# Second MLP of a linear-attention block: x forms kept in an SBUF ring, second-layer weights stored column-permuted, last sums combined in PSUM, other step places

## The chip, the core and the metric

The kernel runs on one core of a Trainium2 chip. The metric is device microseconds of one execution. TensorE (PE) does the matrix work, VectorE (DVE) and ScalarE (ACT) empty PSUM and do elementwise work, GpSimd (POOL) does elementwise work in SBUF, and SyncE (SP) issues nearly all DMAs.

## The reference

```python
x = attention(q, k, v)                         # linear attention, 4608 tokens x 512
x = (relu(x @ moe_w_in) ** 2) @ moe_w_out      # first MLP, 512 -> 2048 -> 512
h = x @ moe2_w_in                              # second MLP, same sizes
g = h * (1.0 / (1.0 + np.exp(-1.702 * h)))
return g @ moe2_w_out
```

Everything is float32. The kernel splits each operand into a high and a low float32r part and adds three matmuls for each product.

## The kernel before

Until about 880 us the kernel does the attention and the first MLP, which leaves its output in DRAM (`y_d`), and it prepares the weights of the second MLP. The change leaves that part alone, but for a few steps that already belong to the second MLP.

The second MLP works in six blocks `i` of 768 tokens (`NB2`) and, for each, eight quads of 256 hidden columns. Quad `n` (0 to 47) belongs to block `n // 8`. Both layers use a seven-product scheme over two-by-two blocks of their operands. Its seven forms are called a11, s2, a12, s3, s1, a22 and s4.

* **First layer.** For each block, `steps_s` makes the seven forms of x: it loads `xf`, does four sums, and for each form writes a high part on ACT (`h.`, through `to_hi`) and a low part on POOL or DVE (`l.`, through `to_lo`). For each quad, `steps_l1` issues seven products of six matmuls each (tiles `pa`, `ps`). Weights come from DRAM through SP, four loads a quad in `load_in` (w1, wa, wb, wq). DVE adds the products (`+c12`, `+c22`, `++c22`, `+c21`, `++c12`), ACT applies the activation, DVE makes the sums `s3'`, `s1'`, `s2'`, `s4'`, and ACT and POOL split them into the tiles `g`.
* **Second layer of block 0.** `unit` multiplies the split g with weights `wo2` (512 columns), quad after quad, between the products.
* **Second layer of blocks 1 to 5, the grid.** A group `k` is two quads. For each form and each output half `t`, `chain(c)` issues six matmuls (tiles `pca`, `pcs`, and `pla`, `pls` for the forms a12 and s4). The chain's weights come from DRAM (`load_out`, tiles `wa`, `ws`). Products and chains alternate on PE, 269 chains beside 269 products, with the last chains alone at the end. `evict(c)` moves a chain's PSUM bank into sums in SBUF: by ACT in the first group of a block, by DVE additions after that. Two banks take turns, so a chain waits for the eviction two chains ahead. Forms a12 and s4 stay in PSUM over a whole block.
* **Output.** `steps_y` adds the sums, transposes them on DVE into `o`, and `put` stores `o`, with 16 DMAs a block, every other one from ACT's queue.

x forms of blocks 1 to 5: four of the seven (a11, s2, a12, s3) are split early into two staging slots, stored to DRAM (`split_x`) and loaded again (`r.` steps) when the block before has read its own; the others are written straight into place. All seven have fixed places:

```python
X_AT = dict(a11="x4", s2="x5", a12="x6", s3="x0", s1="x1", a22="x2", s4="x3")
```

The order of all this is a list of steps with planned times, `plan`, sorted by time. Each engine, and SP's queue too, runs its instructions in that order.

Of the kernel before, what the change touches and what calls it, by code (L numbers as in the profile page):

```python
# [8 lines left out]
F32 = mybir.dt.float32  # L9
# [47 lines left out]
CHANGE = """  # L57
"""


@with_exitstack
def kernel(
# [29 lines left out]
    nc = tc.nc  # L92
# [59 lines left out]
    def at(t, label, fn, *args):  # L152
# [8 lines left out]
    FORMS = ("a11", "a22", "s3", "s2", "s1", "s4", "a12")  # L161
    LASTING = ("a12", "s4")
# [6 lines left out]
    split_x = {  # L169
        (i, a): dram.tile([P, 2, 2, TH], F32, name=f"x{a}{i}") for i in range(1, NB2) for a in ("a11", "s2", "a12", "s3")  # L170
    }
# [159 lines left out]
    def steps_t(n):  # L331
# [19 lines left out]
        def split(e):  # L351
            def run():
                w = wpool.tile([P, 2, DM], F32R, tag=slots[e], name=f"wt{n}_{e}")
                to_hi(w[:, 0, :], st["t"][:, e, :])
                to_lo(w[:, 1, :], st["t"][:, e, :], w[:, 0, :], nc.gpsimd)
# [423 lines left out]
    def to_late():  # L779
# [5 lines left out]
    X_AT = dict(a11="x4", s2="x5", a12="x6", s3="x0", s1="x1", a22="x2", s4="x3")  # L785
# [10 lines left out]
    SUMS = dict(a11=(14,), a22=(15, 0), s3=(16, 1), s1=(17, 2), s2=(18,))  # L796
    G_AT = dict(
        a11=(19, 20), a22=(21, 22), s3=(23, 24), s1=(25, 26), s2=(27, 30, 31), a12=("g",), s4=(28, 29, "g4")
    )

    def g_tile(x, n):
        at = G_AT[x][(n - NQ) % len(G_AT[x])]
        pool, tag = {"g": (gpool, "g"), "g4": (late["pool"], "g4")}.get(at) or (wpool, slots[at])
        return pool.tile([P, 2, TH], F32R, tag=tag, name=f"g{x}_{n}")
# [11 lines left out]
    def load_out(k, x):  # L816
        at = (len(FORMS) * k + FORMS.index(x)) % len(W_OUT)
        w = wpool.tile([P, 2, 2, HC], F32R, tag=slots[W_OUT[at]], name=f"w{x}_{k}")
        wt["s", x, k] = w
        nc.sync.dma_start(out=w.bitcast(F32), in_=split_o[k % (NQ // 2), x])  # L820

    def steps_s(i):
# [25 lines left out]
        def split(a, src, eng):  # L848
            def hi():
                if i and a in ("a11", "s2", "a12", "s3"):  # L850
                    st["x", a] = [wpool.tile([P, 2, TH], F32R, tag=slots[4 + e], name=f"{a}{e}_{i}") for e in range(2)]
                else:
                    st["x", a] = xpool.tile([P, 2, 2, TH], F32R, tag=X_AT[a], name=f"{a}_{i}")
                    st["x", a] = [st["x", a], st["x", a][:, 0], st["x", a][:, 1]]
                to_hi(st["x", a][-2], src())

            def lo():
                *x, hi_, lo_ = st["x", a]
                to_lo(lo_, src(), hi_, eng)
                if x:  # L860
                    x_t["2", i, a] = x[0]
                    return
# [34 lines left out]
    def steps_l1(n):  # L897
# [5 lines left out]
        def product(at, x, begin):  # L903
            def run():
# [4 lines left out]
                for k in range(2):  # L909
# [4 lines left out]
                        lambda e: xs[:, e, k, :],  # L914
# [85 lines left out]
        if i == 0:  # L1000
# [16 lines left out]
            return steps  # L1017
        late_done = max(done(6), done(5) + 2.0)
# [41 lines left out]
    def put_2(tokens, acc):  # L1060
        if tokens not in (0, 5):
            o = late["pool"].tile([P, TB], F32, tag="o", name=f"o2_{tokens}", bufs=2)
        else:
            if not more_o:
                more_o[0] = cpool.tile([P, 2, TB], F32, tag="raw", name="o2")
            o = more_o[0][:, tokens // 5, :]
        if tokens % 2 == 0:
            nc.scalar.activation(o, acc, AF.Copy)
        else:
            nc.vector.tensor_copy(o, acc)  # L1070
# [5 lines left out]
    totals = {}  # L1076

    def chain_of(c):
        k, m = divmod(c, NX)
        i, at = divmod(k, GROUPS)  # L1080
        return 1 + i, k, at, FORMS[m // 2], m % 2

    def chain(c):
# [3 lines left out]
        if not lasting:  # L1087
            totals["ps", c] = late_ps["pool"].tile([P, TB], F32, tag=f"acc{4 + c % 2}", name=f"pc{x}_{c}")
        elif at == 0:
            totals[i, x, t] = ps_acc.tile([P, TB], F32, tag=f"acc{2 * LASTING.index(x) + t}", name=f"pl{x}{t}_{i}")  # L1090
        bank = totals[i, x, t] if lasting else totals["ps", c]
        w = wt["s", x, k].rearrange("p e h (d t) -> p e h t d", t=2)
        for e in range(2):
            g = g_t["2", NQ + 2 * k + e, x]
            three(
                bank[:, :TH],
                lambda h: w[:, e, h, t],
                lambda h: g[:, h, :],
                e == 0 and (at == 0 or not lasting),
                e == 1 and (at == GROUPS - 1 or not lasting),  # L1100
# [3 lines left out]
    def evict(c):  # L1104
        i, k, at, x, t = chain_of(c)
        if at == 0 and t == 0:
            if x == "a11" and i % 2 == 0:
                pool, tag = cpool, "raw"
            else:
                pool, tag = wpool, slots[SUMS[x][(i - 1) % len(SUMS[x])]]  # L1110
# [7 lines left out]
    def steps_y(i):  # L1118
# [4 lines left out]
        def add(out, x, y):  # L1123
            return lambda: nc.vector.tensor_tensor(out=both(out), in0=both(x), in1=both(y), op=ALU.add)
# [16 lines left out]
        def put(row, col, q):  # L1141
            def run():
                r0, c = (2 * i + row) * TH, col * HC + 64 * q
                (nc.sync if q % 2 else nc.scalar).dma_start(
# [10 lines left out]
            "c22": add("s3", "s3", "s1"),  # L1155
            "u4": add("s1", "s2", "s1"),
        }
        for name, x, of, row, col in (("12", "s1", "s4", 0, 1), ("11", "a11", "a12", 0, 0)):
# [9 lines left out]
    with tc.manual_schedule():  # L1168
# [108 lines left out]
        grid = second_half + 6 * UT  # L1277
        SLOT = 2.09
# [18 lines left out]
        for i in range(NB2):  # L1297
# [6 lines left out]
            else:  # L1304
                on = lambda n, dt: product_at(NQ * (i - 1) + n, 0) + dt
                e = lambda n: product_at(NQ * i - 1, n) + PT
                if i == 1:
                    times = [on(4, 6.0), on(5, 2.0), on(5, 4.0), on(6, 1.0), on(7, 1.0)]
                    times += [on(5, 0.0), on(5, 0.8), e(0) + 0.2]
                    times += [on(6, 3.0), on(6, 4.0), e(1) + 0.2]  # L1310
                    times += [on(5, 8.0), on(5, 8.8), e(2) + 0.2]
                    times += [on(6, 9.0), on(6, 10.0), e(3) + 0.2]
                else:
                    times = [on(3, 9.0), on(4, 7.9), on(4, 9.75), on(5, 3.5), on(7, 5.5)]
                    times += [on(4, 11.5), on(4, 12.7), e(0) + 0.2]
                    times += [on(5, 5.0), on(5, 5.5), e(1) + 0.2]
                    times += [on(6, 6.5), on(6, 7.9), e(2) + 0.2]
                    times += [on(7, 3.0), on(7, 3.5), e(3) + 0.2]
                times += [e(4) + 0.4, e(4) + 1.2, e(5) + 0.4, e(5) + 1.2, e(6) + 0.4, e(6) + 1.2]
# [17 lines left out]
        for c in range((NB2 - 1) * GROUPS * NX):  # L1337
            i, group, e, x, t = chain_of(c)
            at(chain_at(c), f"c{c}", chain, c)
            if x not in LASTING:  # L1340
# [4 lines left out]
        for i in range(1, NB2):  # L1345
# [9 lines left out]
            else:  # L1355
                at_y = dict(u2=7, u3=7.1, c21=7.2, o100=7.3, o101=7.4, c22=9, u4=9.2, o110=9.4, o111=9.6)
                at_y.update(c120=10, c121=11, o010=10.5, o011=11.5, c110=12, c111=13, o000=12.5, o001=13.5)
                times = {e: t(int(y)) + PT * (y % 1) for e, y in at_y.items()}
                for e, y in dict(d10=7.5, d11=9.7, d01=11.6, d00=13.6).items():
                    times.update({f"{e}{q}": t(int(y)) + PT * (y % 1 + 0.01 * q) for q in range(4)})  # L1360
# [3 lines left out]
        plan.sort(key=lambda e: e[:2])  # L1364
        order = CHANGE.split()
        at_change = [n for n, e in enumerate(plan) if e[2] in set(order)]
        by_label = {plan[n][2]: plan[n][3:] for n in at_change}
        assert len(order) == len(at_change) == len(by_label)
        for n, label in zip(at_change, order):
            plan[n] = (plan[n][0], n, label, *by_label[label])  # L1370
# [32 lines left out]
```

## Time and profile before

| | us |
|---|---|
| median of 3 runs | 1640.59 (1638.63 to 1643.13) |
| the profiled execution, its own time | 1639.32 |
| its span, first to last instruction | 1637.2 |
| outside the span | 2.1 |
| PE busy | 1599.8, 98% of the span |
| DVE, ACT, POOL busy | 1058.1, 740.1, 856.1 |
| read from HBM, written | 246.42 MB, 72.35 MB |

A busy PE here means that a matmul is in flight; since matmuls are pipelined, a longer distance between their starts hides in the busy time. Rows of a timeline give the start of a run of equal instructions, how long it lasted, and in brackets how long the engine had stood idle before and what ended that.

### The profile page before, as it was taken

How to read it: one execution, taken by the hardware profiler on the slowest of the kernel's cores; microseconds unless marked ns; L12 is line 12 of the kernel's file. 1: busy time of each engine (PE TensorE's matmuls, PEld its weight loads, DVE VectorE, ACT ScalarE, POOL GpSimd, SP SyncE). 2: the span in 40 equal slices, each digit the busy share in tenths (PEclk: the TensorE clock that was granted, in tenths of full speed). 3: DMA queues.
4: the chain of work that ended last, by engine and by line, in shares of the span. 5: the costliest groups of instructions: out<-in, count | busy, mean ns of one | idle time of the engine just before them, and what ended most of it. 6: DMA issues, size and time to landing. Idle time of an engine off the chain costs nothing.

```text
span 1637.2 us, 23437 instructions
## 1 busy us (share of the span) xinstructions
PE 1599.8 (98%) x8084; PEld 1431.0 (87%) x8084; DVE 1058.1 (65%) x1866; ACT 740.1 (45%) x1402; POOL 856.1 (52%) x727
## 2 busy tenths in 40 slices
PE   7999999999999999999999999999999999999997
PEld 5888888888888888888888898999999999999996
DVE  7967777676776767656456332576666666667656
ACT  5874444444444444433435444544444444444432
POOL 6764333433433343343478684676576575576453
PEclk9999999999999999999999999999999999999998
DMA  9642232223323222121254798899899999899974
GB/s 267 214 127 86 66 107 80 81 88 98 100 67 107 81 62 86 60 77 52 95 221 181 262 306 279 290 376 356 278 329 353 289 325 339 285 323 362 281 251 136
DMA packets 211158, 320.32 MB, mean 196 GB/s; under 512 B 86880, under 2 KB 138080, under 8 KB 211040
## 3 DMA queue, kind: packets, MB, share of 16 engines
q1 hardware_dynamic: 192368, 311.48, 56.6%
q10 hardware_dynamic: 18672, 7.34, 1.8%
q8 instruction: 64, 1.05, 0.3%
q14 instruction: 54, 0.44, 0.1%
HBM read 246.42 MB, written 72.35 MB: 195 GB/s over the span
## 4 chain that ended last, share of the span: by engine, by line
PE 83%; DVE 6%; DMA 5%; ACT 2%; issue 2%; POOL 1%; SPq 1%; ACTq 0%; DVEq 0%; POOLq 0%
PE acc L714 24%; PE ph L714 22%; PE ps L714 13%; PE pcs L714 7%; PE pa L714 5%; PE pca L714 4%; PE pla L714 2%; PE pls L714 2%; DMA w<-wiw 2%; PE pk L527 2%; PE px L669 2%; DMA to<-wod 1%; DVE qt L624 1%; DVE c L957 1%; DVE s L957 1%
## 5 line engine op out<-in xcount | busy, mean ns | idle before, releaser
L714 PE MATMUL ph<-x,wi 128*128 128x512 f32 x1728 | 422.1, 393 | 0.2
L714 PE MATMUL acc<-g,wo 128*128 128x512 f32 x1728 | 418.6, 391 | 0.1
L146 POOL TENSOR_TENSOR g<-g,g 128x512 fp32r<-128x512 f32 x144 | 192.2, 1335 | 379.7 <-ACT g L143 336.2
L714 PEld LDWEIGHTS ph<-x,wi 128*128 128x128 f32 x1728 | 320.9, 188 | 68.3 <-issue 0.7
L714 PEld LDWEIGHTS acc<-g,wo 128*128 128x128 f32 x1728 | 321.8, 188 | 67.0 <-DVE to L231 0.6
L146 POOL TENSOR_TENSOR ga<-c,ga 128x384 fp32r<-128x384 f32 x120 | 130.2, 1087 | 129.7 <-ACT ga L143 99.0
L143 ACT ACTIVATE g<-g 128x512 fp32r<-128x512 f32 x144 | 91.0, 632 | 207.0 <-DVE g L741 206.9
L741 DVE TENSOR_TENSOR g<-g 128x512 f32<-128x512 f32 x128 | 108.4, 847 | 114.7 <-ACT g L735 111.2
L938 DVE TENSOR_TENSOR c<-ps,m 128x384 f32<-128x384 f32 x144 | 79.9, 555 | 157.5 <-PE ps L714 142.8
L735 ACT ACTIVATE g<-ph 128x512 f32<-128x512 f32 x144 | 85.6, 595 | 164.5 <-PE ph L714 162.0
L714 PE MATMUL pcs<-gs,ws 128*128 128x384 f32 x720 | 144.5, 337 | 3.1 <-ACT sums L1114 2.3
L624 DVE STREAM_TRANSPOSE qt<-q 32x128 f32<-32x128 f32 x448 | 135.5, 302 | 5.7
L947 ACT ACTIVATE c<-c 128x384 f32<-128x384 f32 x144 | 75.2, 522 | 137.4 <-DVE c L938 137.4
L146 POOL TENSOR_TENSOR gs<-s,gs 128x384 fp32r<-128x384 f32 x80 | 99.5, 1243 | 70.2 <-ACT gs L143 65.8
L714 PEld LDWEIGHTS pcs<-gs,ws 128*128 128x128 f32 x720 | 126.9, 194 | 6.1 <-ACT sums L1114 4.8
L714 PE MATMUL pa<-a,w 128*128 128x384 f32 x576 | 119.8, 343 | 5.4 <-DVE c L938 1.9
L714 PE MATMUL ps<-s,wa 128*128 128x384 f32 x576 | 118.8, 342 | 1.3 <-DVE c L938 1.3
L714 PEld LDWEIGHTS pa<-a,w 128*128 128x128 f32 x576 | 103.3, 189 | 9.0 <-DVE c L957 3.6
L714 PEld LDWEIGHTS ps<-s,wa 128*128 128x128 f32 x576 | 103.7, 190 | 3.4 <-DVE c L938 1.7
L146 POOL TENSOR_TENSOR gs<-c,gs 128x384 fp32r<-128x384 f32 x80 | 93.4, 1182 | 10.9 <-ACT gs L143 5.7
L714 PE MATMUL pca<-ga,wa 128*128 128x384 f32 x480 | 96.7, 338 | 0.0
L714 PEld LDWEIGHTS pca<-ga,wa 128*128 128x128 f32 x480 | 85.9, 196 | 0.0
(149 smaller groups left out, 2551.5 us busy)
## 6 DMA issues: line engine op xcount, KB each, us to landing
ws<-wos SPq DMA_DIRECT2D x80, 512.0 KB, 5.3
wa<-woa SPq DMA_DIRECT2D x60, 512.0 KB, 5.3
wq<-wiwq SPq DMA_DIRECT2D x40, 512.0 KB, 5.9
w<-wiw SPq DMA_DIRECT2D x40, 512.0 KB, 5.1
wa<-wiwa SPq DMA_DIRECT2D x40, 512.0 KB, 5.3
rawo<-in_moe_w_out_dram SPq DMA_DIRECT2D x30, 512.0 KB, 3.8
rawi<-in_moe_w_in_dram SPq DMA_DIRECT2D x28, 512.0 KB, 4.3
wb<-wiwb SPq DMA_DIRECT2D x40, 256.0 KB, 4.7
```

The costliest lines, as they stand in the source:

```text
L143: nc.scalar.activation(hi, src, AF.Copy)
L146: eng.tensor_tensor(out=lo, in0=src, in1=hi.bitcast(F32), op=ALU.subtract)
L527: nc.tensor.matmul(st["pk"][:, :VW], st["ke"][:, j, :], st["v"][:, j, :], start=(j == 0), stop=(j == KJ),)
L624: nc.vector.transpose(out=st["qt"][32 * g : 32 * g + 32, a * P : (a + 1) * P].rearrange("d (j t) -> d j t", j=QJ), in_=st["qn"][32 * a : 3 ...
L669: nc.tensor.matmul(st["px"][:, cols], a, c[:, cols], start=(e == 0), stop=(e == 2))
L714: nc.tensor.matmul(out, w(a), x(b), start=(start and e == 0), stop=(stop and e == 2), skip_group_check=shared)
L735: nc.scalar.activation(st["g"], st["h"], AF.Relu)
L741: nc.vector.tensor_tensor(out=st["g"], in0=st["g"], in1=st["g"], op=ALU.mult)
L938: nc.vector.tensor_tensor(out=st[name], in0=st[at][:, :TH], in1=other, op=ALU.add)
L947: nc.scalar.activation(st[name], h, AF.Gelu_apprx_sigmoid)
L957: nc.vector.tensor_tensor(out=st[out], in0=st[a], in1=st[b], op=op)
```

## The change

* The x forms of blocks 1 to 5 no longer pass through DRAM. They are written once, into a ring of ten SBUF places, seven x places and three pairs of weight slots. `split_x`, its 20 times two stores and 20 loads are gone. The g tiles get their places from a table of when each place comes free (14 places, 17 before).
* The second-layer weights are stored with their even columns first and then the odd ones of each half (`even_odd`), so that a chain's 128 weight columns are neighbours where they were every second column. The splits of these weights now read every second column, and block 0's output is put back in order as it leaves PSUM (`put_2`).
* In the last group, chains whose sums are added anyway accumulate in the same PSUM bank (`END_ADDS`), the other additions are made earlier, and two of them go to POOL.
* Output DMAs all go to SP's queue, but for the last block.
* The places of many steps move by a table of offsets in us (`SHIFT`), with keys by kind and quad.

```diff
+SHIFT = """
+b.h.a11-1.04 b.h.a12-10.42 b.h.a22-1.12 b.h.s1+0.45 b.h.s2+0.25 b.h.s4+1.49 b.l.a11+0.31 b.l.a12-0.17
...
+    def even_odd(t):
+        return t.rearrange("p (h m t) -> p h t m", h=2, t=2)
+
+    def split_even_odd(w, src):
+        hi_, lo_ = (w[:, e, :].rearrange("p (h t m) -> p h t m", h=2, t=2) for e in range(2))
+        to_hi(hi_, even_odd(src))
+        to_lo(lo_, even_odd(src), hi_, nc.gpsimd)
...
-                to_hi(w[:, 0, :], st["t"][:, e, :])
-                to_lo(w[:, 1, :], st["t"][:, e, :], w[:, 0, :], nc.gpsimd)
+                split_even_odd(w, st["t"][:, e, :])
...
+    X_ORDER = ("a11", "s2", "a12", "s3", "s1", "a22", "s4")
+    X_PLACES = ("x4", "x5", "x6", "x0", "x1", "x2", "x3", (4, 5), (14, 15), (16, 17))
...
-                for e in range(2):
-                    nc.sync.dma_start(out=split_x[i, a][:, e], in_=st["x", a][e].bitcast(F32))
-
-            def again():
-                x = x_t["2", i, a] = xpool.tile([P, 2, 2, TH], F32R, tag=X_AT[a], name=f"{a}_{i}")
-                nc.sync.dma_start(out=x.bitcast(F32), in_=split_x[i, a])
...
+    END_ADDS = dict(
+        a11=("a11",), a22=("a22",), s2=("s1",), s3=("a22", "s3"), s1=("s3",), s4=("s1",), a12=("a11",)
+    )
...
-        w = wt["s", x, k].rearrange("p e h (d t) -> p e h t d", t=2)
+        w = wt["s", x, k].rearrange("p e h (t m) -> p e h t m", t=2)
...
-                (nc.sync if q % 2 else nc.scalar).dma_start(
+                (nc.scalar if q % 2 and i == NB2 - 1 else nc.sync).dma_start(
...
-        plan.sort(key=lambda e: e[:2])
+        plan.sort(key=lambda e: (e[0] + moved.get(shift_key(e[2]), 0.0), e[1]))
```

Three places show how instructions move. The first is SP's queue where block 1 hands over to block 2, around the load of w1 for quad 16; `a11_2` and its like are x forms of block 2, `xa11` and `xs3` their copies in DRAM, `ws` and `wa` chain weights. Before:

```order
L814 DMA wq_16_10318<-wiwq0_143 128x1024
L868 DMA a11_2_10332<-xa112_191 128x1536
L868 DMA s2_2_10358<-xs22_192 128x1536
L864 DMA xs32_194<-s30_2_10347 128x768
L864 DMA xs32_194<-s31_2_10348 128x768
L820 DMA ws3_3_10370<-wos33_182 128x1024
L814 DMA w1_16_10380<-wiw10_127 128x1024
L868 DMA a12_2_10382<-xa122_193 128x1536
L868 DMA s3_2_10402<-xs32_194 128x1536
```

The same place of SP's queue in the changed kernel:

```order
L876 DMA wq_16_10274<-wiwq0_143 128x1024
L882 DMA ws3_3_10311<-wos33_182 128x1024
L876 DMA w1_16_10339<-wiw10_127 128x1024
L882 DMA ws2_3_10352<-wos23_183 128x1024
L876 DMA wa_16_10374<-wiwa0_135 128x1024
```

The two reloads and two stores ahead of w1, and the two reloads behind it, are gone.

The second place is ACT in quads 17 and 18, where block 1 is put out; `out_0_dram<-o1` is a store of block 1, `sums3_2<-pcs3_60` an eviction of chain 60. Before:

```order
L1144 DMA out_0_dram<-o1_10796 32x12x64
L1114 ACTIVATE suma22_2_10810<-pca22_59_10819 128x384
L1144 DMA out_0_dram<-o1_10796 32x12x64 x2
L1114 ACTIVATE sums3_2_10872<-pcs3_60_10850 128x384
L947 ACTIVATE c11_18_10881<-pa11_18_10803 128x384
L1144 DMA out_0_dram<-o1_10796 32x12x64 x2
L143 ACTIVATE ga11_18_10889<-c11_18_10881 128x384
L1114 ACTIVATE sums3_2_10872<-pcs3_61_10874 128x384
```

The same place of ACT in the changed kernel:

```order
L1188 ACTIVATE suma22_2_10755<-pca22_59_10767 128x384
L1188 ACTIVATE sums3_2_10816<-pcs3_60_10797 128x384
L1188 ACTIVATE sums3_2_10816<-pcs3_61_10821 128x384
L1000 ACTIVATE c11_18_10833<-pa11_18_10748 128x384
L196 ACTIVATE ga11_18_10865<-c11_18_10833 128x384
```

The stores have left ACT. On SP's queue of the changed kernel they stand like this, between chain weights and the loads for quad 19:

```order
L876 DMA wq_19_10759<-wiwq3_146 128x1024
L1220 DMA out_0_dram<-o1_10717 32x12x64 x4
L882 DMA ws4_4_10793<-wos40_164 128x1024
L1220 DMA out_0_dram<-o1_10717 32x12x64 x8
L876 DMA w1_19_10835<-wiw13_130 128x1024
```

There were four stores on SP ahead of `w1_19`, and now there are twelve.

The third place is DVE's end; `pla120` and `pla121` are the banks of the last two chains, `o5` the output tile. Before, from the eviction of chain 274 on:

```order
L1116 TENSOR_TENSOR sums1_5_14936<-pcs1_274_15777,sums1_5_14936 128x384
L1116 TENSOR_TENSOR sums1_5_14936<-pcs1_275_15795,sums1_5_14936 128x384
L1124 TENSOR_TENSOR sums3_5_14844<-sums3_5_14844,sums1_5_14936 128x768
L1124 TENSOR_TENSOR sums1_5_14936<-sums2_5_14895,sums1_5_14936 128x768
L1135 STREAM_TRANSPOSE o5_15788<-sums3_5_14844 128x384 x2
L1127 TENSOR_TENSOR sums1_5_14936<-pls40_5_14975,sums1_5_14936 128x384
L1135 STREAM_TRANSPOSE o5_15788<-sums1_5_14936 128x384
L1127 TENSOR_TENSOR sums1_5_14936<-pls41_5_14997,sums1_5_14936 128x384
L1135 STREAM_TRANSPOSE o5_15788<-sums1_5_14936 128x384
L1127 TENSOR_TENSOR suma11_5_14726<-pla120_5_15015,suma11_5_14726 128x384
L1135 STREAM_TRANSPOSE o5_15788<-suma11_5_14726 128x384
L1127 TENSOR_TENSOR suma11_5_14726<-pla121_5_15035,suma11_5_14726 128x384
```

In the changed kernel, also from chain 274 on (the bank `pvs10`):

```order
L1180 TENSOR_TENSOR sums3_5_14734<-pvs10_15675,sums3_5_14734 128x384
L1211 STREAM_TRANSPOSE o5_15673<-sums3_5_14734 128x384
L1180 TENSOR_TENSOR sums3_5_14734<-pvs11_15685,sums3_5_14734 128x384
L1211 STREAM_TRANSPOSE o5_15673<-sums3_5_14734 128x384
L1180 TENSOR_TENSOR sums1_5_14826<-pvs10_15675,sums1_5_14826 128x384
L1211 STREAM_TRANSPOSE o5_15673<-sums1_5_14826 128x384
L1180 TENSOR_TENSOR sums1_5_14826<-pvs11_15685,sums1_5_14826 128x384
L1211 STREAM_TRANSPOSE o5_15673<-sums1_5_14826 128x384
L1180 TENSOR_TENSOR suma11_5_14614<-pla120_5_14906,suma11_5_14614 128x384
L1211 STREAM_TRANSPOSE o5_15673<-suma11_5_14614 128x384
L1180 TENSOR_TENSOR suma11_5_14614<-pla121_5_14927,suma11_5_14614 128x384
L1211 STREAM_TRANSPOSE o5_15673<-suma11_5_14614 128x384
```

Each of the last six chains is now followed on DVE by one addition and one transpose; the 768-wide additions between have gone to earlier places.

## Rows read from the trace of the kernel before

**Rows 1.** Waits of PE, 835 us to the end: total us, times, longest.

```profile
PE ps L714 <- DVE c L938: 4.6, 4, 2.3
PE pcs L714 <- ACT sums L1114: 2.3, 4, 0.8
PE pa L714 <- DVE c L938: 1.9, 1, 1.9
PE pa L714 <- DMA w<-wiw: 1.6, 2, 0.8
PE pa L714 <- DVE c L957: 1.2, 1, 1.2
PE acc L714 <- POOL wo L146: 1.1, 2, 0.8
PE pa L714 <- ACT m L931: 0.7, 1, 0.7
```

**Rows 2.** Timeline of PE in the grid: start us, us, instructions.

```profile
1085.54 1.23 PE L714 MATMUL pa<-a,w 128*128 128x384 f32 x6
1086.61 1.20 PE L714 MATMUL pls<-gs,ws 128*128 128x384 f32 x6
1087.65 1.23 PE L714 MATMUL ps<-s,wq 128*128 128x384 f32 x6
```

**Rows 3.** Timeline of PE in block 0, products that follow one another.

```profile
893.87 1.20 PE L714 MATMUL ps<-a,wq 128*128 128x384 f32 x6
894.91 1.21 PE L714 MATMUL ps<-s,wbb 128*128 128x384 f32 x6
```

**Rows 4.** Timeline of PE in the first MLP, its two layers in turn.

```profile
867.62 2.88 PE L714 MATMUL acc<-g,wo 128*128 128x512 f32 x12
870.34 2.88 PE L714 MATMUL ph<-x,wi 128*128 128x512 f32 x12
```

**Rows 5.** Weight loads by shape, 1085 to 1115 us: count | busy us, mean ns.

```profile
L714 PEld LDWEIGHTS pcs<-gs,ws 128*128 128x128 f32 x39 | 6.9, 194 | 0.0
...
L714 PEld LDWEIGHTS ps<-s,wa 128*128 128x128 f32 x24 | 4.3, 188 | 0.0
```

**Rows 6.** Timeline of PE where blocks 2 and 4 begin.

```profile
1128.74 1.20 PE L714 MATMUL pca<-ga,wa 128*128 128x384 f32 x6
1130.75 1.30 PE L714 MATMUL pa<-a,w 128*128 128x384 f32 x6 [0.81 <-DMA w<-wiw]
1131.89 1.20 PE L714 MATMUL pca<-ga,wa 128*128 128x384 f32 x6
...
1372.50 1.99 PE L714 MATMUL pa<-a,w 128*128 128x384 f32 x6 [1.88 <-DVE c L938]
1374.29 2.09 PE L714 MATMUL pca<-ga,wa 128*128 128x384 f32 x6
```

**Rows 7.** Windows: us, busy (instructions) of five engines, clock, DMA share, GB/s.

```profile
1010.00:1018.00 8.00, 5.43 (x21) 5.11 (x21) 2.46 (x4) 4.02 (x9) 8.00 (x7) 0.79 0.51 158
1372.00:1380.00 8.00, 7.50 (x34) 7.53 (x35) 4.31 (x6) 2.81 (x7) 6.53 (x6) 0.79 1.00 387
```

**Rows 8.** Landing times of all loads of w1, 1100 to 1600 us.

```profile
DMA to landing us min/median/max: 3.9/5.0/10.3
```

**Rows 9.** Timeline of ACT in quad 7, the split of weights o7.

```profile
1006.68 0.63 ACT L143 ACTIVATE wo<-to 128x512 fp32r<-128x512 f32 x1 [6.88 <-DMA to<-wod]
```

**Rows 10.** ACT's splits by shape, 300 to 700 us: mean ns.

```profile
L143 ACT ACTIVATE g<-g 128x512 fp32r<-128x512 f32 x66 | 41.8, 633 | 105.7 <-DVE g L741 105.7
...
L143 ACT ACTIVATE qh<-qt 128x512 fp32r<-128x512 f32 x17 | 18.8, 1107 | 0.0
```

**Rows 11.** Timeline of all engines at the end.

```profile
1624.03 2.24 PE L714 MATMUL pla<-ga,wa 128*128 128x384 f32 x12
...
1628.45 0.52 DVE L1127 TENSOR_TENSOR sums<-pls,sums 128x384 f32<-128x384 f32 x1
...
1632.17 0.58 DVE L1135 STREAM_TRANSPOSE o<-suma 128x384 f32<-128x384 f32 x1
```

More of the change, by code (lines that the diff above doesn't have):

```diff
@@ L1 @@
+import re
 from contextlib import ExitStack
@@ L795 @@
     W_OUT = (10, 11, 12, 13)
[L796 to L799, printed above, removed]
+    SUM_ORDER = ("a11", "a22", "s3", "s2", "s1")
+    SUM_PLACES = (18, 19, 20, 21, None, 0, 1, 2)
     def g_tile(x, n):
[L802 to L803 removed]
+        till = chain_at(NX * ((n - NQ) // 2) + 2 * forms((n - NQ) // 2).index(x) + 1) + PT
+        at = min(g_free, key=g_free.get)
+        if g_three[0] <= g_free[at]:
+            g_three.pop(0)
+            g_three.append(till)
+            return gpool.tile([P, 2, TH], F32R, tag="g", name=f"g{x}_{n}")
+        g_free[at] = till
+        pool, tag = (late["pool"], "g4") if at == "g4" else (wpool, slots[at])
         return pool.tile([P, 2, TH], F32R, tag=tag, name=f"g{x}_{n}")
@@ L1076, with forms @@
     totals = {}
+    def forms(k):
+        return END_FORMS if k == (NB2 - 1) * GROUPS - 1 else FORMS
     def chain_of(c):
@@ L1086, in chain @@
         lasting = x in LASTING
[L1087 to L1091, printed above, removed]
-        w = wt["s", x, k].rearrange("p e h (d t) -> p e h t d", t=2)
+        begin, end = at == 0 or not lasting, at == GROUPS - 1 or not lasting
+        if k == (NB2 - 1) * GROUPS - 1 and x != "a12":
+            begin, end = x in ("a11", "a22", "s1"), x not in ("a11", "s2", "s1")
+            if x == "a11":
+                totals["end", t] = late_ps["pool"].tile([P, TB], F32, tag=f"acc{4 + t}", name=f"pu{t}")
+            elif begin:
+                totals["end", 2 + t] = ps_acc.tile([P, TB], F32, tag=f"acc{2 + t}", name=f"pv{x}{t}")
+            to = totals["end", t + (0 if x in ("a11", "s2", "s3") else 2)]
+        elif lasting:
+            if at == 0:
+                totals[i, x, t] = ps_acc.tile([P, TB], F32, tag=f"acc{2 * LASTING.index(x) + t}", name=f"pl{x}{t}_{i}")
+            to = totals[i, x, t]
+        else:
+            to = totals["ps", c] = late_ps["pool"].tile([P, TB], F32, tag=f"acc{4 + c % 2}", name=f"pc{x}_{c}")
+        w = wt["s", x, k].rearrange("p e h (t m) -> p e h t m", t=2)
         for e in range(2):
@@ L1095, in chain @@
             three(
-                bank[:, :TH],
+                to[:, :TH],
                 lambda h: w[:, e, h, t],
                 lambda h: g[:, h, :],
-                e == 0 and (at == 0 or not lasting),
-                e == 1 and (at == GROUPS - 1 or not lasting),
+                e == 0 and begin,
+                e == 1 and end,
                 shared=True,
@@ L1105, in evict @@
         i, k, at, x, t = chain_of(c)
+        if k == (NB2 - 1) * GROUPS - 1:
+            bank = totals[i, x, t] if x == "a12" else totals["end", t + (0 if x in ("a11", "s2", "s3") else 2)]
+            for name in END_ADDS[x]:
+                o = totals[i, name][:, t]
+                nc.vector.tensor_tensor(out=o, in0=bank[:, :TH], in1=o, op=ALU.add)
+            return
         if at == 0 and t == 0:
[L1107 to L1110, printed above, removed]
+            place = SUM_PLACES[(len(SUM_ORDER) * (i - 1) + SUM_ORDER.index(x)) % len(SUM_PLACES)]
+            pool, tag = (cpool, "raw") if place is None else (wpool, slots[place])
             totals[i, x] = pool.tile([P, 2, TH], F32, tag=tag, name=f"sum{x}_{i}")
@@ L1121, in steps_y, with add @@
         both = lambda x: totals[i, x]
-        def add(out, x, y):
-            return lambda: nc.vector.tensor_tensor(out=both(out), in0=both(x), in1=both(y), op=ALU.add)
+        def add(out, x, y, eng=nc.vector):
+            return lambda: eng.tensor_tensor(out=both(out), in0=both(x), in1=both(y), op=ALU.add)
+        other = nc.vector if i < NB2 - 1 else nc.gpsimd
         def add_ps(out, x, t):
@@ L1154, in steps_y @@
             "c21": add("a22", "s3", "a22"),
-            "c22": add("s3", "s3", "s1"),
-            "u4": add("s1", "s2", "s1"),
+            "c22": add("s3", "s3", "s1", other),
+            "u4": add("s1", "s2", "s1", other),
         }
-        for name, x, of, row, col in (("12", "s1", "s4", 0, 1), ("11", "a11", "a12", 0, 0)):
+        for name, x, of in (("12", "s1", "s4"), ("11", "a11", "a12")) if i < NB2 - 1 else (("12", "s2", "s4"),):
             for t in range(2):
@@ L1277 @@
         grid = second_half + 6 * UT
+        g_free = {at: grid if at in (*range(28, 32), "g4") else 0.0 for at in (*range(22, 2 * NF), "g4")}
+        g_three = [grid] * 3
         SLOT = 2.09
@@ L1339 @@
             at(chain_at(c), f"c{c}", chain, c)
-            if x not in LASTING:
+            if x not in LASTING or group == (NB2 - 1) * GROUPS - 1:
                 at(chain_at(c) + PT + 0.1, f"e{c}", evict, c)
```

131 lines of the change are left out of this document (82 added, 49 removed).

## The prediction

> **What bounds the kernel.** I read the page first: PE is busy for 98% of the span, so no other engine's busy time can be the end. The gain, if there is one, has to come out of PE's waits, out of the distance between PE's instructions, or out of what follows PE's last one. I therefore read the list of PE's waits, PE's timeline for distances, and the end of all engines.
>
> PE's waits in the second MLP are few: the groups shown add up to 13.4 us out of 800 [rows 1]. The distance between starts tells more than the busy time, since matmuls overlap: in the grid a product takes 1085.54 to 1086.61, 1.07 us, and the chain behind it 1.04 [rows 2]. Both are six matmuls of the same shape. A product that follows a product takes 1.04 too [rows 3], which is 173.3 ns a matmul. So the odd 0.03 us belongs to a product that comes behind a chain. Alternation alone doesn't do it: in the first MLP two layers, both with neighbouring weight columns, take turns, and twelve matmuls take 2.72 us, 226.7 ns each with four thirds of the columns, as even as it can be [rows 4]. The chains' weights differ in one thing, that they read every second column, and their weight loads take 194 ns where a product's take 188 [rows 5].
>
> The last matmul ends at 1624.03 + 2.24 = 1626.27, and DVE's last transpose at 1632.75 [rows 11], 6.5 us later. The last stores take the rest, to 1637.2.
>
> **The change, term by term.** No matmul goes, and the order on PE hardly moves. So the sum is made of distances, waits and the tail, against the profiled execution's 1639.3, which lies 1.3 below the median of the three runs.
>
> *Neighbouring columns.* If the strided weight load is what makes the next product late, 269 products fall from 1.07 to 1.04, seen over the pair as 2.11 to 2.08 [rows 2, 3]: 269 x 0.027 = **7.3 us**. The bounds: nothing, if the extra 0.03 comes from something else in a chain (its moving tile, its bank), and 8 us the other way, if a product's and a chain's distance both became 1.07. I take the upper end because the chain and the product differ in nothing else that rows 3 and 4 do not already excuse. [...]
>
> *Block starts.* Each of blocks 2 to 5 begins with a wait for its first products' operands: 0.8 and 0.8 for w1, and 1.9 and 1.2 that the list puts down to DVE [rows 1, 6]. I take all four to be one thing. The load of w1 stands on SP's queue behind reloads and stores of x, as the first order listing shows, and loads of w1 land 3.9 to 10.3 us after their issue, 5.0 in the middle [rows 7, 8]: the DMA engines are full there (share 1.00, 387 GB/s where block 4 begins). Without reloads, w1 stands in the program's order at least seven PE blocks of 1.05 us ahead of its product, 7.3 us, for a landing of 5. Gain 1.6 + 1.9 + 1.2 = **4.7**.
>
> *ACT's evictions.* PE waits 2.3 in four places for `sums` from ACT [rows 1]; there ACT issues stores between evictions, as the second listing shows. They leave ACT: **2.3**. The price is on SP, twelve stores ahead of `w1_19` instead of four; it belongs to the rivals.
>
> *Weights o7.* ACT stood 6.88 us for the load of o7 [rows 9], and PE behind it for the 2.3 that is the longest of DVE's and for ACT's 0.7 (`m`) [rows 1]. Its load no longer queues behind x traffic, and its step comes earlier: **3.0**. If the load were late again, nothing of it would be won.
>
> *DVE and POOL in single quads.* Other waits for DVE are 4.6 - 2.3 = 2.3 and for `wo` from POOL 1.1 [rows 1]. Steps move there by tenths of a microsecond. I credit two thirds, 1.5 + 0.7 = **2.2**; the bounds are 0 and 3.4.
>
> *Restarts.* A wait costs more than its idle time. At 1130.75 the chain before should have handed over at 1128.74 + 1.04 = 1129.78; PE is 0.97 late where the wait reads 0.81, and the first product takes 1.14 instead of 1.07 [rows 6]: 0.23 extra. Some 13 waits go, so **3.0**.
>
> *Half clock.* [...] At 1372.50 a product is busy 1.99 instead of 1.30 and the chain behind it 2.09 instead of 1.20 [rows 6]: 1.6 us, say 1.5 without the restart. Two stretches: **3.0**. [...]
>
> *The tail.* DVE does eight operations from 1628.45 to 1632.75, 0.54 each [rows 11]. In the changed kernel 18 stand from the eviction of chain 272 on (the last twelve are in the listing): 9.7 us. PE meanwhile has seven chains, 7.3 us. DVE thus ends 9.7 - 7.3 = 2.4 after the last matmul, not 6.5: **4.1**. The bounds are 5.4, since one addition and one transpose (1.1) must follow the last chain, and 0, if POOL's two additions came late and held DVE.
>
> *Costs that I put at nothing.* Splitting a weight with every second column read may slow ACT, at worst as far as a permuted split, 1.11 us against 0.63 [rows 10]; 32 such splits would be 15 us of ACT, spread over the stretch before the grid. ACT is busy for half of 1010 to 1018 [rows 7], which hides it; uncovered, one delayed quad is 0.5 us. The x forms need the ring's old tile to be free, and the g tiles share 14 places where they had 17; in the program's order the last reader of a place stands six PE blocks or more ahead of its next writer, some 6 us, and that covers them. Should one be late, ACT or POOL stands, and behind it the other splits of the quad, for which PE's chains wait.
>
> *New waits.* A new order has misfits of its own. The bounds are 0 and today's 13; I charge **4**, about a third, since nothing is left of the traffic that made the largest ones. It includes the last group, where s2's low part on POOL now comes just before its chain.
>
> Sum: 7.3 + 4.7 + 2.3 + 3.0 + 2.2 + 3.0 + 3.0 + 4.1 - 4 = 25.6. 1639.3 - 25.6 = 1613.7, and 1.3 for the median gives **1615**.
>
> **Rivals.**
>
> *The column order gives nothing.* For it: the chain itself shows no loss [rows 2]. Against it: the evenness in rows 3 and 4. The rest stands, so 1615 + 7 = **1622**. [...]
>
> *Waits change places.* Twelve stores and the chain weights now stand ahead of `w1_19` on one queue, and five blocks pass there. If a load is late as at 1130.75, that costs 1 us with its restart, and where it grows to 1.9 us another 1.5 of half clock. For it: the longest landings reach 10.3 [rows 8]. Against it: those fell where reloads filled the engines. Two such waits a block, ten in all, some 10 to 15 us: about **1630**.
>
> *Slower: DVE is held in each quad.* `++c12` waits for the last product of its quad; if it now stands ahead of a sum that the next chain's tile needs, DVE's queue stands and PE with it. For 39 quads in the grid the loss passes the 25.6 won from 0.66 us a quad; at 0.8 it is 31, **1646**. Against it: in the trace of before, DVE's waits on PE are single ones, and the moves here are mostly under 1 us.
>
> *Nothing to see.* Gain and new waits cancel, each some 20 us: about **1640**.
>
> **How the numbers follow.** Likeliest 0.58, no column gain 0.22, waits change places 0.10, slower 0.05, nothing 0.05. The likeliest one's own range is 1608 to 1621: below, no charge (4), all of the single quads (1.2), 8 for the columns (0.7) and the best tail (1.3); above, no credit for single quads (2.2) and a charge of 8. The whole range, 1605 to 1631, reaches over the second case and its own spread into the third, which leaves out about 2 in 10. What a measurement can tell from no change is 0.3%, 5 us. The first three cases lie more than that under 1640.6: faster 0.90, same 0.05, slower 0.05.
>
> **What would show it.** Right: a product in the grid takes 1.04, and product and chain 2.08; no wait for w1 where blocks begin, its longest landing under 7 us; no wait for `sums` from ACT; a clock of 1.00 from 1000 us on; DVE's last transpose 2 to 3 us after the last matmul; no DMA of x copies. Wrong: products still at 1.07 (the first rival); waits for `w` in the middle of blocks with stores ahead on SP (the second); a wait for DVE in every quad (the third). What would make the number wrong with the steps right is the charge of 4, which rests on no row.

## The result and the profile after

| | before | after |
|---|---|---|
| median | 1641.09 us (1638.63 to 1643.13) | 1611.28 us (1611.03 to 1611.42) |
| ratio after / before | | 0.9819 (0.9802 to 0.9836) |
| span of the profiled execution | 1637.2 | 1609.3 |
| start of the first product | 881.2 | 882.4 |
| second MLP, first product to end of span | 756.0 | 726.9 |
| read from HBM, written, MB | 246.42, 72.35 | 230.69, 56.62 |

Faster by 29.8 us; 1615 was forecast, with 1605 to 1631 as the range. The first part of the kernel is the same in both, yet its last microseconds fall a little differently in each execution (the first product starts between 880.2 and 884.1 us in the runs below), so the second MLP's own length is the better measure: 29.1 us less.

PE's waits, as in [rows 1] (us in total, times, longest):

```profile
PE pa L771 <- DMA w<-wiw: 1.1, 2, 0.7
PE pu L771 <- ACT gs L196: 0.9, 1, 0.9
PE acc L771 <- POOL wo L199: 0.7, 1, 0.7
PE pu L771 <- POOL gs L199: 0.6, 1, 0.6
PE pa L771 <- DVE c L991: 0.5, 1, 0.5
PE pvs L771 <- DVE sums L1180: 0.3, 1, 0.3
PE ps L771 <- DVE c L991: 0.2, 1, 0.2
```

They add up to 4.3 us where the groups of [rows 1] have 13.4. Nothing is left at block starts; the 1.1 for w1 is in quads 19 and 35, two of the four places where the twelve stores stand ahead of the load. There w1 is issued 4.1 us ahead of its product's start, at the other two 4.6 and 4.8, at block starts 9.2. It lands after 3.9 and 4.0, so it is late because it was issued late. Three waits (`pu`, `pvs`, 1.8 us) are new and lie in the last group.

PE's timeline in the grid, as in [rows 2]:

```profile
1084.16 1.20 PE L771 MATMUL ps<-s,wa 128*128 128x384 f32 x6
1085.20 1.20 PE L771 MATMUL pla<-ga,wa 128*128 128x384 f32 x6
1086.24 1.20 PE L771 MATMUL ps<-s,wa 128*128 128x384 f32 x6
```

Product and chain take 1.04 us each, the pair 2.08 (mean of some 250 pairs of the grid without waits: 2.082, before 2.113). The weight loads, as in [rows 5], 1085 to 1115 us (count | busy, mean ns):

```profile
L771 PEld LDWEIGHTS pcs<-gs,ws 128*128 128x128 f32 x36 | 6.3, 188 | 0.0
L771 PEld LDWEIGHTS ps<-s,wa 128*128 128x128 f32 x25 | 4.4, 188 | 0.0
```

A chain's load now takes what a product's does. Windows of the changed kernel (columns as in [rows 7]): 420 us of the grid, block 2's beginning, and the stretch that had a granted clock of 0.79 before [rows 7]:

```profile
1060.00:1480.00 420.00, 418.91 (x2415) 418.21 (x2415) 281.26 (x446) 202.02 (x407) 271.95 (x228) 1.00 0.84 281
1115.00:1135.00 20.00, 20.00 (x118) 20.00 (x117) 13.40 (x24) 8.17 (x17) 14.16 (x11) 1.00 0.73 244
1010.00:1018.00 8.00, 8.00 (x42) 7.29 (x41) 5.24 (x8) 4.25 (x9) 3.06 (x4) 1.00 0.89 272
```

The first two of the kernel before, for comparison:

```profile
1060.00:1480.00 420.00, 413.81 (x2336) 410.67 (x2335) 278.02 (x432) 191.25 (x389) 266.29 (x219) 1.00 0.93 326
1115.00:1135.00 20.00, 19.19 (x110) 18.91 (x109) 14.84 (x21) 11.40 (x22) 14.76 (x12) 1.00 0.99 375
```

The DMA engines (last column but one) were full where a block begins (0.99), and now have a quarter to spare (0.73). The landing times of w1, as in [rows 8]:

```profile
DMA to landing us min/median/max: 3.5/4.5/7.3
```

And the end, as in [rows 11]:

```profile
1601.22 2.24 PE L771 MATMUL pla<-ga,wa 128*128 128x384 f32 x12
...
1604.27 0.58 DVE L1211 STREAM_TRANSPOSE o<-suma 128x384 f32<-128x384 f32 x1
```

PE's last matmul ends at 1603.46, DVE's last transpose at 1604.85: 1.4 us later, where it was 6.5.

### The profile page after: what moved, and what is told of

Read it like the earlier page. It is cut to its first block, busy times and chain, and to the rows that moved or that the text cites. A ratio compares the mean times of both kernels' runs of the same rounds, so it can differ in the third digit from the quotient of the medians.

```text
span 1609.3 us, 23330 instructions
## 1 busy us (share of the span) xinstructions
PE 1586.0 (99%) x8084; PEld 1422.0 (88%) x8084; DVE 1045.2 (65%) x1868; ACT 742.7 (46%) x1402; POOL 853.2 (53%) x729
## 3 DMA queue, kind: packets, MB, share of 16 engines
q8 instruction: 64, 1.05, 0.3%
HBM read 230.69 MB, written 56.62 MB: 179 GB/s over the span
## 4 chain that ended last, share of the span: by engine, by line
PE 89%; DVE 4%; DMA 2%; issue 2%; ACT 1%; SPq 1%; POOL 1%; DVEq 0%; POOLq 0%; ACTq 0%
PE acc L771 26%; PE ph L771 22%; PE ps L771 14%; PE pcs L771 7%; PE pa L771 6%; PE pca L771 5%; PE pla L771 2%; PE pls L771 2%; PE pk L584 2%; PE px L726 2%; DVE qt L681 1%; DMA w<-wiw 0%; DMA rawi<-in_moe_w_in_dram 0%; DMA kt<-in_k_dram 0%; DMA to<-wod 0%
## 5 line engine op out<-in xcount | busy, mean ns | idle before, releaser
L199 POOL TENSOR_TENSOR ga<-c,ga 128x384 fp32r<-128x384 f32 x120 | 129.2, 1085 | 120.1 <-ACT ga L196 74.4
L771 PE MATMUL pcs<-gs,ws 128*128 128x384 f32 x684 | 136.9, 334 | 0.1
L771 PEld LDWEIGHTS pcs<-gs,ws 128*128 128x128 f32 x684 | 120.1, 188 | 0.4 <-ACT suma L1188 0.4
L771 PE MATMUL pa<-a,w 128*128 128x384 f32 x576 | 115.7, 335 | 1.6 <-DMA w<-wiw 1.1
L771 PE MATMUL ps<-s,wa 128*128 128x384 f32 x576 | 115.4, 335 | 0.0
L199 POOL TENSOR_TENSOR gs<-s,gs 128x384 fp32r<-128x384 f32 x80 | 94.8, 1185 | 34.1 <-ACT gs L196 21.5
L771 PE MATMUL pca<-ga,wa 128*128 128x384 f32 x456 | 91.2, 334 | 0.0
L771 PEld LDWEIGHTS pca<-ga,wa 128*128 128x128 f32 x456 | 80.1, 188 | 0.0
```

The source lines that it names most:

```text
L199: eng.tensor_tensor(out=lo, in0=src, in1=hi.bitcast(F32), op=ALU.subtract)
L771: nc.tensor.matmul(out, w(a), x(b), start=(start and e == 0), stop=(stop and e == 2), skip_group_check=shared)
```

## The experiments

Times are medians, beside the ratio to runs of the kernel before on the same chip, with its interval. Differences to the changed kernel are between medians of different sets of runs; the kernel before had medians of 1641.1, 1639.9, 1639.1 and 1638.4 us in these sets, so such a difference is uncertain by 2 to 3 us; by the ratios they come out 1 to 3 us larger.

### The weight columns alone, taken back

```diff
-        w = wt["s", x, k].rearrange("p e h (t m) -> p e h t m", t=2)
+        w = wt["s", x, k].rearrange("p e h (m t) -> p e h t m", t=2)
```

> The changed kernel, whose chains read every second weight column again; the output columns come in another order, nothing else differs. If the stride is what makes the product behind a chain 0.027 us longer: pairs of 2.107 instead of 2.080 us, 269 of them, +7.3 us, about 1618.6. If every second column is read at full speed and the 7 us came from elsewhere: 1611.3.

1617.70 us, 0.9868 (0.9837 to 0.9899): 6.4 over the changed kernel. Its timeline of PE in the grid, and then its weight loads from 1085 to 1115 us:

```profile
1085.34 1.23 PE L771 MATMUL pa<-a,w 128*128 128x384 f32 x6
1086.40 1.20 PE L771 MATMUL pla<-ga,wa 128*128 128x384 f32 x6
1087.44 1.23 PE L771 MATMUL ps<-s,wa 128*128 128x384 f32 x6
```

```profile
L771 PEld LDWEIGHTS pcs<-gs,ws 128*128 128x128 f32 x36 | 6.4, 194 | 0.0
L771 PEld LDWEIGHTS ps<-s,wa 128*128 128x128 f32 x24 | 4.3, 188 | 0.0
```

The pair is back at 2.10 (mean over the grid 2.111), with the product behind the chain the longer one, and the load at 194 ns. The chain's access is the only thing that differs, so the stride alone makes the pair longer.

### Every fourth column

```diff
-        w = wt["s", x, k].rearrange("p e h (t m) -> p e h t m", t=2)
+        w = wt["s", x, k].rearrange("p e h c -> p e (h c)").rearrange("p e (m h t) -> p e h t m", h=2, t=2)
```

> The changed kernel, whose chains read every fourth column of the high and low part together, so the products have other values and the work is the same. By the stride theory the product behind a chain is late by 0.027 us or more: 1618.6 or above. [...]

1708.46 us, 1.0417 (1.0386 to 1.0449): 97 over the changed kernel. The same two views of this kernel, one after the other:

```profile
1084.96 1.22 PE L771 MATMUL pa<-a,w 128*128 128x384 f32 x6
1086.01 1.56 PE L771 MATMUL pls<-gs,ws 128*128 128x384 f32 x6
1087.41 1.22 PE L771 MATMUL ps<-s,wq 128*128 128x384 f32 x6
```

```profile
L771 PEld LDWEIGHTS pcs<-gs,ws 128*128 128x128 f32 x24 | 5.9, 327 | 0.0
L771 PEld LDWEIGHTS ps<-s,wa 128*128 128x128 f32 x24 | 4.3, 191 | 0.0
```

Now it is the chain that takes longer, 1.40, and its loads take 327 ns, where matmuls had started every 173. The matmuls of the chain start every 233 ns, less than a load's 327, so the loads overlap in part; what sets the 233 is not shown. The pair is 2.45 us, and 269 x 0.37 = 100 us is about what the time shows. The stride theory holds for the time, and for the place only in part: nearly all of the loss is in the chain itself, and the product behind it takes 1.05. Against neighbouring columns the load is 1.74 times as long with every fourth (327 against 188 ns), and with every second 6 ns longer (194): that is small, but it isn't nothing, for 269 pairs made some 7 us of it.

### Neighbouring columns in the kernel before

The same edit as the change's, in the chain alone: `(d t)` became `(t d)` in its weight access.

> The kernel before, whose chains read neighbouring columns; the output columns come in another order, nothing else differs. Stride theory: pairs of 2.080 us, 7.3 us less, about 1633.8, with the waits as they were. Rival, that the even pairs came with the new places: 1641.

1635.17 us, 0.9964 (0.9948 to 0.9979): 4.8 less between the medians, 3.4 to 8.5 by the interval, which has room for the 7.3. PE's largest wait in it:

```profile
PE pa L714 <- DVE c L938: 7.1, 4, 2.0
```

All four block starts now wait for 1.6 to 2.0 us, where [rows 1] has 0.8 to 1.9. That is 2.4 us more than before (7.1 against 4.7): PE came earlier, and what it waits for there hardly did. So the gain was real, and in the profiled execution the block starts took 2.4 us of it back.

### The kernel before without x traffic

```diff
-                for e in range(2):
-                    nc.sync.dma_start(out=split_x[i, a][:, e], in_=st["x", a][e].bitcast(F32))
+                return
 
             def again():
-                x = x_t["2", i, a] = xpool.tile([P, 2, 2, TH], F32R, tag=X_AT[a], name=f"{a}_{i}")
-                nc.sync.dma_start(out=x.bitcast(F32), in_=split_x[i, a])
+                x_t["2", i, a] = x_t["2", 0, a]
```

> The kernel before without the stores and the reloads of the x copies: the four forms concerned are multiplied from block 0's tiles in all blocks, all places of steps stay. If the traffic made the load of w1 late, the waits at four block starts go: 4.7 us with 0.9 of restarts and 1.5 of half clock, and if it made the weights o7 late too, another 3.0, 0.5 and 1.5: 7 to 12 us less, 1629 to 1634. Rival, that DVE's places made the waits that the profile puts down to it (1.9, 1.2 and 2.3 us): only the two of 0.8 go, about 1639.

1627.16 us, 0.9921 (0.9895 to 0.9948): 12.8 less than before's 1639.94. All of PE's waits of 0.4 us and more:

```profile
PE ps L714 <- DVE c L936: 2.2, 3, 1.6
PE pcs L714 <- ACT sums L1112: 2.0, 5, 0.6
PE pa L714 <- ACT m L929: 0.7, 1, 0.7
PE pcs L714 <- DVE suma L1114: 0.6, 2, 0.5
PE pa L714 <- DVE c L936: 0.4, 1, 0.4
```

No block start waits any more, also not where the profile of before names DVE, and of o7's 2.3 us 0.2 is left (in the 2.2; the 1.6 is in quad 0). No step of DVE's was moved, so DVE was not the cause. The 0.7 for `m` stays, so that one was not the traffic's.

Which DMA came last, w1 or a reload of x, the trace of the kernel before tells. Its loads of w1 for blocks 3 and 4, where the list names DVE, are issued here:

```profile
1241.90 0.84 SPq L814 DMA_DIRECT2D w<-wiw  x1
1362.09 0.46 SPq L814 DMA_DIRECT2D w<-wiw  x1
```

They land 9.7 and 10.3 us later, at 1251.6 and 1372.4, and the products that use them start at 1251.74 and 1372.50. For blocks 2 and 5 the sums are 1130.6 and 1494.1, for starts at 1130.75 and 1494.26. The reload of a11 for block 4 had landed at 1366.2. So w1 came last at all four block starts, and the rival is out.

### The traffic in the changed kernel

```diff
+                if i and a in ("a11", "s2", "a12", "s3"):
+                    for e in range(2):
+                        nc.sync.dma_start(out=split_x[i, a][:, e], in_=st["x", a][e].bitcast(F32))
...
+            def again():
+                nc.sync.dma_start(out=again_x[i, a], in_=split_x[i, a])
...
+                for j, (a, again) in enumerate(extra):
+                    at(e(j) + 0.2, f"r{i}.{a}", again)
```

> The changed kernel with the traffic put back that it saves: after each low part of the four forms two stores from the ring to DRAM, and where the reloads stood a copy of the same bytes, from DRAM to DRAM, that nothing reads. If the traffic made w1 late wherever it stands: waits for w1 at four or five block starts, 5 to 7 us, 1616 to 1618. If the earlier places of the loads alone took the waits away: 1611 to 1612.

1643.83 us, 1.0029 (1.0017 to 1.0042): 32.5 over the changed kernel, far more than either theory had, and more than the whole change gave. PE's two largest waits, and then its timeline at the beginning of block 2:

```profile
PE pa L778 <- DMA w<-wiw: 16.1, 6, 4.1
PE ps L778 <- DVE c L1007: 4.8, 2, 4.6
```

```profile
1136.17 2.26 PE L778 MATMUL pa<-a,w 128*128 128x384 f32 x6 [4.04 <-DMA w<-wiw]
1138.23 2.12 PE L778 MATMUL pca<-ga,wa 128*128 128x384 f32 x6
```

The wait is 4 us, and a stretch at half clock follows it (0.50 granted from 1136 to 1140 us, a product 2.06 us to the next start). So the new order does not protect against this traffic. At the four block starts w1 is issued 6.6 to 7.0 us before PE is ready for it, and lands after 10.0 to 10.9. In the kernel before these were 8.2 to 8.7 and 8.9 to 10.3, in the changed kernel the lead is 9.2. Against the kernel before these waits are 2.7 us longer in the mean: 1.7 of that is the shorter lead, w1 being issued behind stores and copies on SP's queue, and 1.0 the later landing. The traffic is also more than what the change saves: 88.08 MB are written to HBM here and 72.35 before, since the copies go to DRAM where the reloads went to SBUF. What each share is worth in the 32.5 was not separated.

The same with the copies in the middle of the block:

```diff
-                    at(e(j) + 0.2, f"r{i}.{a}", again)
+                    at(product_at(NQ * i + 3, j) + PT + 0.2, f"r{i}.{a}", again)
```

> The changed kernel with the x traffic put back as in the run with stores and copies, but the copies 3 quads later, in the middle of the block. With them at the hand-over PE waited 16.1 us for w1, nearly all at block starts, and the time was 1643.8. If it is the crowd at the hand-over (x loads, stores, copies and weights at once): most of the four waits of 4 us go, 1615 to 1625. If it is the bytes as such, wherever they stand: the waits move with them, 1635 and above.

1648.63 us, 1.0065 (1.0048 to 1.0083). The largest wait, and then the landing times of w1:

```profile
PE pa L778 <- DMA w<-wiw: 21.5, 6, 4.6
```

```profile
DMA to landing us min/median/max: 3.5/5.3/12.3
```

The waits went along with the copies: none is left at a block start, and five of 3.6 to 4.6 us stand where the copies are. My idea of a crowd that belongs to the hand-over is wrong: at both places tried, with copies of 0.8 MB each near a w1 on this queue, its landing (11.4 to 12.3 us at these five) goes beyond its lead of 6.9 to 8.8.

### Stores on ACT again

```diff
-                (nc.scalar if q % 2 and i == NB2 - 1 else nc.sync).dma_start(
+                (nc.sync if q % 2 else nc.scalar).dma_start(
```

> The changed kernel with every other store of the output issued by ACT in all blocks, as before. If the issues on ACT held the evictions: the four waits of 2.3 us come back, with 0.9 of restarts, 1614.5. If the new places leave ACT room for them: 1611.3.

1622.00 us, 0.9900 (0.9876 to 0.9923): 10.7 more, three times the 3.2 expected. PE's largest wait, ACT's timeline in quad 18, and PE's behind it, in this order:

```profile
PE ps L771 <- ACT c L1000: 7.2, 4, 2.0
```

```profile
1159.43 2.43 ACTq L1220 DMA_DIRECT2D out_dram<-o  x2
1161.91 0.49 ACT L1188 ACTIVATE sums<-pcs 128x384 f32<-128x384 f32 x1 [2.79 <-DMA ws<-wos]
1162.21 0.32 ACTq L1220 DMA_DIRECT2D out_dram<-o  x1
1162.30 0.48 ACT L1000 ACTIVATE c<-pa 128x384 f32<-128x384 f32 x1
```

```profile
1162.84 1.32 PE L771 MATMUL ps<-s,wa 128*128 128x384 f32 x6 [1.87 <-ACT c L1000]
```

Two issues hold ACT for 2.43 us. Behind them stand an eviction of a chain and then `c11`, which empties the bank of a product; in the new order it is the latter that PE waits for, 1.9 us at three of the four outputs and 1.4 at the fourth.

### An empty table of offsets

`SHIFT` empty, nothing else.

> The changed kernel with an empty table of offsets: every step at its planned time. The prediction credited 2.2 us to moves in single quads and nearly all else to what left the queues, so by it 2 to 5 us more, 1613 to 1616. Rival: the table is what makes the rest work, and without it PE waits as much as before or more, by 15 us or more: 1626 and above.

1622.35 us, 0.9899 (0.9880 to 0.9917): 11.1 more, between the two theories. Its two largest waits:

```profile
PE ps L739 <- DVE c L959: 4.7, 9, 1.3
PE acc L739 <- POOL wo L167: 3.5, 2, 3.3
```

Its second MLP is 12.8 us longer, and 8.1 of that lie before block 1's first product (1012.9 - 880.6 against 1006.6 - 882.4). The longest wait is there, 3.3 us, with the granted clock at 0.50 for the 4 us behind it: POOL, after standing for 5.5 us, splits a form of x and a `wt` ahead of the `wo` that PE needs. The kernel before, in its own order, doesn't have this one.

### The old tail

The last group is as before: forms in the old order, each chain in its own bank, sums on DVE at the end.

> The changed kernel with the last group as before: each chain in a bank of its own, the sums at the end on DVE. The changed tail ends 1.4 us after the last matmul on DVE where it ended 6.5 us after it, and its group waits some 2.5 us of PE that the group before did not all have. If both count: 3 to 4 us more, 1614 to 1615. If the tail's gain counts alone: 5.1 more, 1616.4. If its end is set by the stores: 1611.3.

1614.72 us, 0.9855 (0.9833 to 0.9878): 3.4 more. Its four runs lie between 1612.2 and 1617.0, so the time alone doesn't tell 3.4 from 5.1. Its trace does: the last matmul and the last transpose are

```profile
1597.20 2.25 PE L771 MATMUL pla<-ga,wa 128*128 128x384 f32 x12
1605.33 0.58 DVE L1211 STREAM_TRANSPOSE o<-suma 128x384 f32<-128x384 f32 x1
```

DVE ends 6.5 us after PE, 5.1 more than in the changed kernel, and from the first chain of the last group to the last matmul's end PE needs 18.1 us, 1.4 less. Both count.

### The parts put together in the kernel before

Without x traffic and with neighbouring columns:

> The kernel before without x traffic and with neighbouring columns, both as in the single runs. The traffic alone gave 12.8 us, the columns alone 4.8, where block starts took part of the 7.3 back. If the rest of the columns' gain was lost to loads that could not come sooner, it is there now: 12.8 + 7.3, about 1620. If both share their gain: 1623 to 1627.

1622.84 us, 0.9909 (0.9892 to 0.9926): 4.3 less than without the traffic alone, at the edge of the second theory. And with the stores of blocks 1 to 4 on SP:

> As the run with both, and the output stores of blocks 1 to 4 all on the SP queue. If the waits for ACT's evictions (2.0 us without x traffic) came from stores on ACT: 2.5 to 3 us less than with both, about 1617. Rival: with the old places twelve stores on SP hold w1 back, and it is no less.

1617.23 us, 0.9877 (0.9862 to 0.9892): 5.6 less than with both, twice the 2.5 to 3 expected. All waits of this one that are 0.3 us or more:

```profile
PE ps L714 <- DVE c L936: 2.1, 4, 1.4
PE pa L714 <- ACT m L929: 0.8, 1, 0.8
PE pcs L714 <- DVE suma L1114: 0.7, 2, 0.5
PE acc L714 <- POOL wo L146: 0.3, 1, 0.3
```

None for `sums` from ACT, and twelve stores on SP hold no load back. Put in a row by the second MLP's length in the profiled executions (end of span less start of the first product):

| kernel | us | step |
|---|---|---|
| before | 1637.2 - 881.2 = 756.0 | |
| no x traffic | 1625.4 - 881.6 = 743.8 | -12.2 |
| and neighbouring columns | 1620.5 - 884.1 = 736.4 | -7.4 |
| and stores on SP | 1615.6 - 883.5 = 732.1 | -4.3 |
| changed kernel with the old tail | 1610.4 - 880.2 = 730.2 | -1.9 |
| changed kernel | 1609.3 - 882.4 = 726.9 | -3.3 |

Each row is one execution. The medians of the same kernels give -4.3, -5.6, -2.5 and -3.4 for the last four steps, so a step is known to 2 or 3 us; the old tail's profiled run was 2.5 us faster than its median, so the last two rows could shift by as much from one to the other. Behind the second row the columns give 7.4; the 4.3 of the medians lacks the later start of the first product (884.1 for 881.6), if the other executions had it too.

### Two places more

```diff
-no.l.s3-0.52 no.s2+0.27 no.s3-0.42 no.s3'+0.11 no.s4+0.86 no.s4'+0.26 o.s0-0.93 o.s1-1.56 o0.ld+2.66
+no.l.s3-0.52 no.s2+0.27 no.s3-0.42 no.s3'+0.11 no.s4+0.86 no.s4'+0.26 o.ld-1.50 o.s0-0.93 o.s1-1.56 o0.ld+2.66
...
-                    times.update({f"{e}{q}": t(0) + SLOT * (y + 0.1 * q - 0.5) for q in range(4)})
+                    times.update({f"{e}{q}": t(0) + SLOT * (y + 0.1 * q - 0.5) + 2.0 for q in range(4)})
```

> The changed kernel with two places moved: the output stores of blocks 1 to 4 2.0 us later, so that fewer stand ahead of w1, and the loads of the weights o2 to o6 1.5 us earlier. The waits for w1 (1.1 us in two) and for wo from POOL (0.7) go with their restarts, about 1609. Rival: the stores meet the next loads instead, and the time stays 1611 or rises.

1609.01 us (1608.31 to 1610.40), 0.9826 (0.9811 to 0.9841). Its largest wait:

```profile
PE ps L771 <- DMA wq<-wiwq: 1.5, 1, 1.5
```

The waits for w1 and for `wo` are gone, and one of 1.5 for wq is there, at 1018 us; the changed kernel has it with 0.1, the runs with every second column and with the traffic have it with 1.5, so it comes and goes without this edit. In us it is the fastest, by its ratio it equals the changed kernel: whether it is better is not settled.

## Why the prediction was right

* **Neighbouring columns**, 7.3: right. 6.4 when taken back, 4.8 and, without the traffic, 7.4 (4.3 by the medians) when added, pairs of 2.08. The 0.027 a pair stands in no row of the prediction, whose rows give 0.03; the means over the grid give 0.031 before and 0.029 when taken back, 8 us. The rival of no gain is out.
* **Block starts and o7**, 4.7 + 3.0 and their share of the restarts and the half clock: right in cause and size. Without traffic 12.2 us of the kernel before went; the terms for these (7.7, six restarts of 0.23, two stretches of 1.5) make 12.1. They are right to about 1 us: ACT's 0.7 and 0.2 of o7 stayed, so the 0.7 that the o7 term counted was not the load's, and as much went elsewhere. That 12.1 and 12.2 agree so closely is luck. No run shows the 3.0 for the half clock apart. What the traces show is a granted clock of 0.50 in the kernel before, from 1014.5 to 1016.5 us behind the wait for o7 and from 1374 to 1376 where block 4 begins, and 1.00 in the changed kernel from 1010 to 1018 and, where its block 4 begins, from 1352 to 1360. What the list put down to DVE was a late load, of w1 or of o7, as I had taken it.
* **ACT's evictions**, 2.3 with about 0.9 of restarts: 4.3 measured (5.6 by the medians). In the new order the same stores would cost 10.7, so the step's worth depends on what stands behind the issues.
* **Single quads**, 2.2, and **new waits**, 4 off: 1.9 came from the table and all other places together, against the same parts in the old order. So these two terms, -1.8 together, were 3 to 4 us too low, by that single row. New waits are the 1.8 in the last group and the 1.1 for w1, some 3 where 4 was charged on no row. An empty table costs 11 us: the ring's order needs its offsets, and the two cannot be valued apart. Of the costs put at nothing, the splits of weights that read every second column took ACT 658 to 663 ns where they had taken 620 to 625, 1.2 us for 32 of them and not the 15 of the worst case.
* **The tail**, 4.1: mis-sized. DVE ends 1.4 after the last matmul, not 2.4: its 18 operations took 9.2 us where 9.7 was counted, and PE took 7.8 beside them where 7.3 was. So 5.1 was won at the end, and 1.5 lost in the group (19.5 us from its first chain to the last matmul's end, 18.0 before), 3.3 in all.
* **Waits change places**: in part, 1.1 us in two of the four blocks with stores ahead of w1, not 10 to 15. The lead of "at least seven PE blocks, 7.3 us" held at block starts (9.2 us) and not behind the stores (4.1). With the stores on SP in the old order there was no such wait.
* **Slower, DVE held in each quad**: did not happen; PE's waits for DVE are three, of 1.0 us together.
* **Signs**: two named for being right missed by a little, w1's longest landing (7.3 us for under 7) and DVE's end (1.4 for 2 to 3); one named for being wrong, a wait for w1 behind stores, is there with 1.1 us.

Together 25.6 were forecast; the span is 27.9 shorter, and the second MLP, which starts 1.2 later in the profiled execution, 29.1. By the table the 3.5 that the forecast lacks are 1.1 in ACT's evictions and some 3 in the single quads, the restarts and the charge, less 0.8 in the tail. The two large terms, columns and traffic, were right in cause and size; the step that was off most is the charge of 4, which rested on no row.

What stays open: how much of the 32 us that the traffic costs in the new order, 12 in the old, comes from w1's shorter lead and how much from the 15.7 MB more that are written, and whether the last kernel is better than the changed one.

## What to carry to other kernels

When PE is busy 98% of the time, look at the distance between starts: 0.03 us in each pair was about a fourth of this gain, and no wait shows it. Where the profile names an engine for a wait at the same place in every block, look at the DMA share there and add issue and landing of the loads that the instruction needs: here the share was 0.99, and a late load stood behind it. Bytes removed were worth more here than a better place, for the waits followed the copies to both places tried (PE waited 16.1 and 21.5 us for w1). Stores issued on ACT cost what stood behind them here: two issues held ACT for 2.43 us, with two PSUM banks to be emptied behind them, and the kernel took 10.7 us more. So put stores on a queue with nothing urgent behind them.

## What the runs showed of the hardware

A weight load of 128 columns took 188 ns with neighbouring float32 columns, 194 with every second and 327 with every fourth. With 194 the chain itself kept its 1.04 us and the product behind it took 1.07: the cost of the longer load showed in the six matmuls behind the chain. With 327 the chain itself took 1.40. A wait of 4 us was followed by a product of 2.06 us, about double (granted clock 0.50 from 1136 to 1140 us in the run with the traffic). All four of that run's waits of 3.3 to 4.1 us at block starts were followed by such a stretch (granted clock 0.50 to 0.68 over 4 us). Of the three waits of 1.9 us with stores on ACT only one, at 1400 us with block 3's output, was (0.58 over 4 us, 1.00 behind the other two); what decides between them was not looked into.
